# Two loads in flight instead of three at the start, and row sums kept in every second column

## The chip, the cores and the metric

One core of a Trainium2 chip runs the whole kernel. The metric is the device time of one execution in microseconds (us), as the median of several runs. The core's engines work side by side, each through its own list of instructions in order: PE (matrix products), DVE and POOL (vectors), ACT (functions and copies), and SP, which here only issues DMA transfers. They wait for each other through semaphores. TensorE and PE are the same engine.

## The reference: what is computed

Two attentions for each of 8 x 8 heads with 576 positions and 64 columns, one over means of four neighbours, one over a narrow band, and their sum goes into a feed-forward layer with `h * cos(h)`:

```python
q_d = q.reshape(B, H, Sd, 4, D).mean(axis=3)         # k_d, v_d alike; Sd = 144
out_up = np.repeat(sm_attn(q_d, k_d, v_d), 4, axis=2)
...
mask = np.abs(pos[:, None] - pos[None, :]) < 4
scores = np.where(mask, scale * q @ k.T, -1e9)
attn = np.exp(scores - max); attn = attn / (np.sum(attn, axis=-1, keepdims=True) + 1e-09)
x = (out_up + attn @ v) reshaped to [4608, 512]
...
h = x @ w_in                                          # w_in [512, 2048]
out = (h * np.cos(h)) @ w_out                         # w_out [2048, 512]
```

The weights arrive as float64 and everything else as float32.

## The kernel before, in words

**The feed-forward layer.** 4608 tokens stand in 12 tiles of 384 columns, the 2048 hidden columns in 16 chunks of 128. For a tile and a chunk, `gemm1` (L741) multiplies in 12 matmuls, each number being split in a high and a low part (h and l in the names), ACT and DVE form `h * cos(h)`, and `gemm2` (L777) adds the product with `w_out` to three PSUM banks in 9 matmuls. The first three tiles take turns, four chunks at a time, and the others come one by one with all 16 chunks.

**The weights.** Each chunk of `w_in` and of `w_out` is loaded by `w_load` (L410, 512 KB, names `wdi` and `wdo`). `w_split` (L420 to L432, then L399) makes float32 high and low parts out of the float64 bits on ACT, DVE and POOL, before gemm1 and gemm2 can read them (`wi`, `wo`).

**The attention.** It runs in 32 units, one for a batch and a pair of heads. A unit has five steps: `u_qk` loads q and k (L476, 292 KB each) and adds groups of four columns for the means (L490 on DVE, or L483 and L485 on POOL); `u_v` loads v twice (L497, 288 KB, names `vd`, and L498, 384 KB, names `vl`) and adds up the first one (L504, L505); `u_s` computes scores on PE (L539, L546, L555), subtracts maxima, applies the exponential and divides by row sums; `u_t` transposes (L634, L650); `u_pv` multiplies with v (L667, L679, L686), and L698, L713 and L399 write the result to the tiles x of the feed-forward layer. The units of the first two batches borrow buffers of weight chunks that come late, so in the rows their tiles carry names such as `wxi`, `wxo` and `xxl`.

**The row sums.** `su` is a tile of 16 columns, allocated in two copies. POOL sets it to 1 (L567). Twelve columns receive the sums of the local attention, four those of the other one (L610, or ACT's accumulator at L597). L612 adds a small number and scales, L614 takes the reciprocal, and L616 (or L622 on ACT) multiplies the rows by it.

**What sets the order.** A planner takes all operations with estimated durations, places them by due time and priority, and the instructions are emitted in that order; each engine follows its own list. Where PE would wait in the first 300 planned microseconds, it gets filling matmuls on an identity matrix (L916).

**The loads in flight.** All loads go out from SP's queue, in order. While the program is written, `dma` adds to each of the first `FIRST` = 40 loads a wait for the load `AHEAD` places before it, unless there is none yet. This dependency is added when the instruction is emitted, behind the planner's back: the planned order doesn't depend on it. SP takes its instructions in order, so a load that waits holds back every later one. The 40 loads are the q, k and v loads of the first two batches, the first four weight chunks in part, and one load of the third batch.

Of the kernel before, what the change touches and what calls it, by code (L numbers as in the profile page):

```python
# [24 lines left out]
P = 128  # L25
# [12 lines left out]
HD = SD // 2  # L38
# [3 lines left out]
NSEG = S // (4 * BQ)  # L42
# [7 lines left out]
ON_PE = ()  # L50
BOOST = {0: 100.0}
LAG = 2
AHEAD, FIRST = 3, 40
PI = math.pi


# [22 lines left out]
class Plan:  # L79
# [47 lines left out]
    def part(self, parent, off, n, make):  # L127

        b = self.buf(make)
        b.parent, b.prev = parent, []  # L130
        for lo, hi, p in parent.parts:
            if lo < off + n and off < hi:
                b.prev.append(p)
        parent.parts = [x for x in parent.parts if not (off <= x[0] and x[1] <= off + n)] + [(off, off + n, b)]
        return b
# [165 lines left out]
def attn_ffn_kernel(ctx: ExitStack, tc: tile.TileContext, qT, kT, vdn, vl, w_in, w_out, out):  # L301
    nc = tc.nc
    pe, act, dve, pool, sp = nc.tensor, nc.scalar, nc.vector, nc.gpsimd, nc.sync
# [6 lines left out]
    pl = Plan()  # L310

    def sb(tag, n, shape, dtype=F32, name=None, pool=None):
        t = pl.turn(tag, n)
        return pl.buf(lambda: (pool or ap).tile(shape, dtype, name=name or tag, tag=t, bufs=1), t)
# [195 lines left out]
    def u_s(b, pr):  # L510
# [49 lines left out]
            pl.op("PE", 1.55, lambda: (l_mm(), d_mm()), r=[q, k, qkd], pw=banks, w=loc + poo)  # L560


        mxl, su = sb("mxl", 2, [P, 2 * NSEG]), sb("su", 2, [P, 2 * NSEG + 4])
        sul = lambda: su.get()[:, :2 * NSEG]
        sud = lambda: su.get()[:HD, 2 * NSEG:].rearrange("p (a b) -> p a b", a=2)

        pl.op("POOL", 0.15, lambda: pool.memset(su.get(), 1.0), w=[su])  # L567
        for h in range(2):
            using(banks[h], pl.op("DVE", _dve(NSEG * BS), lambda h=h: dve.tensor_tensor(  # L569
                out=sml.get()[:, NSEG * h:NSEG * (h + 1)], in0=banks[h].get()[:, LQ:LQ + NSEG * BS].rearrange("p (s n) -> p s n", n=BS),  # L570
# [9 lines left out]
        for h in range(2):  # L580
            mx = pl.buf(None)
            using(banks[h], pl.op("DVE", _dve(2 * SD), lambda h=h: dve.tensor_reduce(
                out=mxd.get()[:, h], in_=dq(h), axis=AX.X, op=ALU.max, negate=early), r=[poo[h]], pw=[mxd], w=[mx]))
            if not early:
                using(banks[h], pl.op("DVE", _dve(2 * SD), lambda h=h: dve.tensor_tensor(
                    out=smd.get()[:, h], in0=dq(h), in1=mxd.get()[:, h].unsqueeze(2).broadcast_to([HD, 2, SD]), op=ALU.subtract),
# [21 lines left out]
        for sm, part, size in ((sml, sul, n), (smd, sud, m)):  # L608
            if not (early and sm is smd):
                pl.op("DVE", _dve(size), lambda sm=sm, part=part: dve.tensor_reduce(  # L610
                    out=part(), in_=sm.get(), axis=AX.X, op=ALU.add), r=[sm, su], pw=[su2])
        pl.op("DVE", 0.1, lambda: dve.tensor_scalar(out=su.get(), in0=su.get(), scalar1=1e-9, scalar2=2.0 * PI,  # L612
                                                    op0=ALU.add, op1=ALU.mult), r=[su2], w=[su])
        pl.op("DVE", 0.15, lambda: dve.reciprocal(su.get(), su.get()), w=[su])  # L614
        for sm, part, size, bc in ((sml, sul, n, bl), (smd, sud, m, bd)):
            f = lambda e, sm=sm, part=part, bc=bc: lambda: e.tensor_tensor(out=sm.get(), in0=sm.get(), in1=bc(part()), op=ALU.mult)  # L616
            alts = [("DVE", _dve(size), f(dve))]
# [193 lines left out]
    def unit(t, step, ahead, *a):  # L811
        for d, f in ((-ahead, u_qk), (0.01 - ahead, u_v), (0.0, u_s), (step, u_t), (2 * step, u_pv)):
            at(t + d, f, *a)

    for i in range(NPAIR):
        for t, f in ((-10.0 + 0.5 * i, u_qk), (-8.4 + 0.5 * i, u_v), (-7.5 + i, u_s), (-6.5 + i, u_t), (-5.5 + i, u_pv)):
            at(t, f, 0, i)
# [15 lines left out]
    for i in range(NPAIR):  # L833
        for t, f in ((-4.0 + 0.5 * i, u_qk), (-2.4 + 0.5 * i, u_v), (-0.9 + i, u_s), (-0.1 + i, u_t), (0.7 + i, u_pv)):
            at(t, f, 1, i)
# [124 lines left out]
```

## Time and profile before

| what | value |
|---|---|
| median of 3 timed runs | 1002.41 us (1001.95 to 1004.67) |
| the profiled execution, its own time | 1007.08 us |
| its span, first to last instruction | 1005.3 us |
| mean granted TensorE clock | 0.988 |
| PE busy | 985.1 us, 98% of the span |
| DVE / ACT / POOL busy | 67% / 61% / 22% |
| DMA moved | 80.70 MB |

The span is what lies between the first and the last instruction of the core; the execution's time has 1.8 us around it. Busy shares are means over stages that differ: in the first 107 us attention units, weight splitting and the first matmuls alternate on PE, later PE multiplies without a pause. In rows of instructions the first number is the start in microseconds from the beginning of the span, the second the duration of the row (of all its instructions together where it ends in x2 or more), then engine, line, operation, output <- inputs with shapes; square brackets hold the idle time of the engine before it and what ended it. Buffer numbers are left out of names.

### The profile page before, as it was taken

The numbers are of one execution on the slowest core, as the hardware profiler recorded it, in microseconds if no ns is written. First come the engines' busy times: TensorE is split into PE (matmuls) and PEld (weight loads), VectorE is DVE, ScalarE is ACT, GpSimd is POOL, SyncE is SP. The second block draws the span as 40 slices with busy tenths as digits, with TensorE's granted clock in tenths as the row PEclk, the third lists the DMA queues.
The fourth block names the chain that finished last, engine by engine and source line by source line (L and its number), as shares of the span: only waits on it lengthen the run. The fifth ranks groups of instructions, "written<-read, shape, count | busy, mean of one in ns | idle before, by whom it ended". The sixth has DMA issues, their size and how long they took to land.

```text
span 1005.3 us, 23882 instructions
## 1 busy us (share of the span) xinstructions
PE 985.1 (98%) x9932; PEld 850.3 (85%) x9932; DVE 678.2 (67%) x1362; ACT 610.2 (61%) x1174; POOL 223.8 (22%) x280
## 2 busy tenths in 40 slices
PE   8898999999998999999999999999999999999998
PEld 5556898899886888889888888888888888899997
DVE  7699999985686678464758957655657765433433
ACT  4357688876665656555547746654646665655554
POOL 6685334631242203000002211200001300000000
PEclk9699999999999999999999999999999999999999
DMA  7874733332453422210212412201112320100000
GB/s 230 250 249 159 255 119 62 72 59 45 75 131 105 84 66 70 66 33 28 82 48 71 127 49 58 82 26 36 64 52 73 116 60 4 37 1 1 32 1 32
DMA packets 41051, 80.70 MB, mean 80 GB/s; under 512 B 4976, under 2 KB 16240, under 8 KB 40944
## 3 DMA queue, kind: packets, MB, share of 16 engines
q1 hardware_dynamic: 37056, 72.11, 23.2%
q0 software_dynamic: 3888, 7.08, 5.0%
q8 instruction: 78, 1.28, 0.5%
q14 instruction: 29, 0.24, 0.1%
HBM read 57.93 MB, written 16.52 MB: 74 GB/s over the span
## 4 chain that ended last, share of the span: by engine, by line
PE 89%; DVE 5%; DMA 1%; issue 1%; ACT 1%; POOL 1%; SPq 0%; ACTq 0%; POOLq 0%; DVEq 0%
PE bank L777 38%; PE bank L741 38%; PE bank L539 2%; PE bank L916 2%; PE bank L686 2%; PE bank L555 2%; PE bank L667 2%; PE bank L650 1%; DMA q<-qT 1%; PE bank L679 1%; DVE su L610 1%; DVE xxh L421 0%; DVE tr L756 0%; PE bank L546 0%; DVE xxh L425 0%
## 5 line engine op out<-in xcount | busy, mean ns | idle before, releaser
L777 PE MATMUL bank<-wo,gh 128*128 128x512 f32 x1152 | 363.9, 397 | 0.0
L777 PEld LDWEIGHTS bank<-wo,gh 128*128 128x128 f32 x1152 | 210.2, 188 | 38.1 <-issue 3.2
L777 PE MATMUL bank<-wo,gl 128*128 128x512 f32 x576 | 227.7, 396 | 0.0
L752 ACT ACTIVATE tr<-bank,bmagic 128x384 f32<-128x384 f32 x192 | 110.9, 578 | 114.1 <-PE bank L741 109.2
L756 DVE SCALAR_TENSOR_TENSOR tr<-tr,bank 128x384 f32<-128x384 f32 x192 | 105.0, 547 | 108.1 <-ACT tr L751 107.4
L753 DVE SCALAR_TENSOR_TENSOR tr<-tr,bank 128x384 f32<-128x384 f32 x192 | 105.7, 551 | 82.8 <-ACT tr L752 81.8
L750 ACT ACTIVATE tr<-tr 128x384 f32<-128x384 f32 x192 | 100.6, 524 | 77.0 <-DVE tr L753 76.4
L758 ACT ACTIVATE gh<-tr 128x384 fp32r<-128x384 f32 x163 | 85.3, 523 | 91.9 <-DVE tr L756 90.1
L399 DVE TENSOR_TENSOR gl<-tr,gh 128x384 fp32r<-128x384 f32 x154 | 91.7, 596 | 63.5 <-ACT gh L758 59.8
L777 PEld LDWEIGHTS bank<-wo,gl 128*128 128x128 f32 x576 | 108.1, 188 | 23.5
L741 PE MATMUL bank<-x3h,wi 128*128 128x384 f32 x384 | 106.9, 338 | 1.6 <-DVE tr L756 1.0
L741 PE MATMUL bank<-x0h,wi 128*128 128x384 f32 x384 | 107.0, 339 | 0.0
L741 PE MATMUL bank<-x1h,wi 128*128 128x384 f32 x384 | 107.0, 339 | 0.0
L741 PE MATMUL bank<-x2h,wi 128*128 128x384 f32 x384 | 106.8, 339 | 0.0
L751 ACT ACTIVATE tr<-tr 128x384 f32<-128x384 f32 x192 | 100.9, 525 | 6.1
L399 POOL TENSOR_TENSOR gl<-tr,gh 128x384 fp32r<-128x384 f32 x38 | 43.3, 1139 | 268.2 <-DVE gh L759 174.7
L741 PEld LDWEIGHTS bank<-x3h,wi 128*128 128x128 f32 x384 | 70.2, 188 | 4.3 <-DVE tr L756 1.5
L741 PEld LDWEIGHTS bank<-x0h,wi 128*128 128x128 f32 x384 | 70.2, 188 | 2.4 <-DVE wxo L569 0.2
L741 PEld LDWEIGHTS bank<-x1h,wi 128*128 128x128 f32 x384 | 70.2, 188 | 2.4 <-issue 0.4
L741 PEld LDWEIGHTS bank<-x2h,wi 128*128 128x128 f32 x384 | 70.2, 188 | 2.2 <-DVE xxh L425 0.2
L741 PE MATMUL bank<-x3l,wi 128*128 128x384 f32 x192 | 64.6, 336 | 0.1
L741 PE MATMUL bank<-x0l,wi 128*128 128x384 f32 x192 | 64.5, 336 | 0.0
(199 smaller groups left out, 1457.2 us busy)
## 6 DMA issues: line engine op xcount, KB each, us to landing
vl<-vl SPq DMA_DIRECT2D x26, 384.0 KB
out<-ob SPq DMA_DIRECT2D x36, 256.0 KB
wdi<-w_in SPq DMA_DIRECT2D x16, 512.0 KB
wdo<-w_out SPq DMA_DIRECT2D x16, 512.0 KB
q<-qT SPq DMA_DIRECT2D x26, 292.0 KB
k<-kT SPq DMA_DIRECT2D x26, 292.0 KB
vd<-vdn SPq DMA_DIRECT2D x26, 288.0 KB
out<-ob POOLq DMA_DIRECT2D x27, 256.0 KB, 5.3
```

The lines of the kernel that those rows point to most:

```text
L399: f = lambda e: lambda: e.tensor_tensor(out=out(), in0=in0(), in1=in1(), op=ALU.subtract)
L539: pe.matmul(banks[h].get()[BS * g:BS * (g + 1), c:c + BS], q.get()[hs, o:o + BS], k.get()[hs, o:o + BS], start=True, stop=True)
L555: pe.matmul(banks[h].get()[:HD, i * SD:(i + 1) * SD], qkd.get()[hs, 0, i * HD:(i + 1) * HD], qkd.get()[hs, 1, :], start=True, stop=True)
L667: pe.matmul(banks[0].get()[64 * h:64 * h + 64, 2 * SD:3 * SD], vd.get()[:, kh, 64 * h:64 * h + 64], ptd.get()[:, h, kh, :], start=(kh == 0 ...
L741: pe.matmul(ph.get()[:, :m], w[:, i, kc, :], x[:, kc, :], start=(n == 0), stop=(n == 3 * KC - 1))
L750: act.activation(tr.get(), tr.get(), AF.Sin, scale=PI)
L751: return act.activation(tr.get(), tr.get(), AF.Square)
L752: pl.op("ACT", _act(m, True, 1), lambda: act.activation(tr.get(), h(), AF.Identity, bias=bmagic), r=[ph], w=[tr])
L753: pl.op("DVE", _dve(m), lambda: dve.scalar_tensor_tensor(out=tr.get(), in0=tr.get(), scalar=MAGIC, in1=h(), op0=ALU.subtract, op1=ALU.subt ...
L756: pl.op("DVE", _dve(m), lambda: dve.scalar_tensor_tensor(out=tr.get(), in0=tr.get(), scalar=0.5, in1=h(), op0=ALU.subtract, op1=ALU.mult), ...
L758: pl.op("ACT", _act(m, False), lambda: act.activation(gh.get(), tr.get(), AF.Copy), r=[tr], w=[gh], alts=[("DVE", _dve(m / 2), lambda: dve ...
L777: pe.matmul(o, (gh, gh, gl)[k].get()[:, sl], wo.get()[:, (0, 1, 0)[k]], start=(c == c0 and k == 0), stop=(c == c1 - 1 and k == 2))
```

## The change

It has two parts. `AHEAD` goes from 3 to 2: each of the first 40 loads waits for the second load before it. And `su` gets a third dimension of 2, so that the 16 sums stand in every second column of a tile of 32; all readers and writers of the sums use the view `every`, and only the memset of POOL writes the whole tile.

```diff
-AHEAD, FIRST = 3, 40
+AHEAD, FIRST = 2, 40
...
-        mxl, su = sb("mxl", 2, [P, 2 * NSEG]), sb("su", 2, [P, 2 * NSEG + 4])
-        sul = lambda: su.get()[:, :2 * NSEG]
-        sud = lambda: su.get()[:HD, 2 * NSEG:].rearrange("p (a b) -> p a b", a=2)
+        mxl, su = sb("mxl", 2, [P, 2 * NSEG]), sb("su", 2, [P, 2 * NSEG + 4, 2])
+        every = lambda: su.get()[:, :, 0]
+        sul = lambda: every()[:, :2 * NSEG]
+        sud = lambda: every()[:HD, 2 * NSEG:].rearrange("p (a b) -> p a b", a=2)
...
-        pl.op("DVE", 0.1, lambda: dve.tensor_scalar(out=su.get(), in0=su.get(), scalar1=1e-9, scalar2=2.0 * PI,
+        pl.op("DVE", 0.1, lambda: dve.tensor_scalar(out=every(), in0=every(), scalar1=1e-9, scalar2=2.0 * PI,
                                                     op0=ALU.add, op1=ALU.mult), r=[su2], w=[su])
-        pl.op("DVE", 0.15, lambda: dve.reciprocal(su.get(), su.get()), w=[su])
+        pl.op("DVE", 0.15, lambda: dve.reciprocal(every(), every()), w=[su])
```

The order of instructions is the same on every engine; the line numbers behind L563 are one higher after the change. What differs is what SP's loads wait for. The loads rotate over eight semaphores, DMAHW0 to DMAHW7, so the number tells which load is waited for. SP's list at its beginning (line, DMA, destination <- source, shape, and what it waits for), before:

```order
L476 DMA q<-qT 128x584
L476 DMA k<-kT 128x584
L476 DMA wxi_132<-qT 128x584
L476 DMA wxo_136<-kT 128x584 [waits DMAHW0_49]
L476 DMA wxo_203<-qT 128x584 [waits DMAHW1_49]
L476 DMA wxi_206<-kT 128x584 [waits DMAHW2_49]
```

and after the change:

```order
L476 DMA q<-qT 128x584
L476 DMA k<-kT 128x584
L476 DMA wxi_132<-qT 128x584 [waits DMAHW0_49]
L476 DMA wxo_136<-kT 128x584 [waits DMAHW1_49]
L476 DMA wxo_203<-qT 128x584 [waits DMAHW2_49]
L476 DMA wxi_206<-kT 128x584 [waits DMAHW3_49]
```

The third load used to go out at once and now waits for the first one (DMAHW0), and each later one waits for one load further on. The same list further down, where the loads of the second batch's v stand (`vd` and `vl` into borrowed tiles; the row with `wxi_312` and `-vdn` is load 32 when the first load is load 0), before:

```order
L410 DMA wdi_925<-w_in 128x4x256 [waits DMAHW1_49]
L410 DMA wdo_934<-w_out 128x1024 [waits DMAHW2_49]
L497 DMA vd_965<-vdn 72x1024 [waits DMAHW3_49,DVE_49,Pool_49]
L498 DMA vl<-vl 128x768 [waits DMAHW4_49,PE_49]
L497 DMA wxi_312<-vdn 72x1024 [waits DMAHW5_49,DVE_49,Pool_49]
```

and after the change:

```order
L410 DMA wdi_925<-w_in 128x4x256 [waits DMAHW2_49]
L410 DMA wdo_934<-w_out 128x1024 [waits DMAHW3_49]
L497 DMA vd_965<-vdn 72x1024 [waits DMAHW4_49,DVE_49,Pool_49]
L498 DMA vl<-vl 128x768 [waits DMAHW5_49,PE_49]
L497 DMA wxi_312<-vdn 72x1024 [waits DMAHW6_49,DVE_49,Pool_49]
```

Here too only the load that is waited for has moved on by one; the waits for DVE, POOL and PE, which free the buffers, are as before.

## The prediction

> **What bounds the kernel now.** First the page: its span, and the chain of work that ended last.
>
> ```profile
> span 1005.3 us, 23882 instructions
> ...
> PE 89%; DVE 5%; DMA 1%; issue 1%; ACT 1%; POOL 1%; SPq 0%; ACTq 0%; POOLq 0%; DVEq 0%
> ```
>
> PE is the chain. Next come the busy times by stretch: start and end, length, then busy time (and instructions) of PE, PE's weight loads, DVE, ACT and POOL, the granted clock, the share of time in which the DMA engines were busy, and GB/s.
>
> ```profile
> 0.75:57.11 56.36, 51.24 (x1058) 32.45 (x1058) 42.00 (x87) 23.08 (x78) 39.02 (x70) 0.82 0.83 243
> 95.00:105.00 10.00, 8.94 (x278) 5.59 (x279) 9.73 (x24) 6.39 (x15) 1.08 (x2) 1.00 0.94 334
> 45.00:50.00 5.00, 5.00 (x21) 2.11 (x18) 3.35 (x6) 1.97 (x5) 4.69 (x9) 0.50 0.82 221
> 107.20:1005.00 897.80, 889.70 (x7896) 787.56 (x7894) 587.17 (x1180) 553.03 (x1011) 153.05 (x173) 1.00 0.24 63
> ```
>
> From 107.2 us on, PE is busy for 889.70 of 897.80 us at full clock: matmul after matmul, in a fixed order. So the question is when PE reaches that stretch; a delay before it goes to the end whole, and nothing behind it can make it up. The 40 loads that the change touches are issued in the first 57 us. There the DMA engines are busy 0.83 of the time but move 243 GB/s, where the unlimited loads around 100 us move 334 GB/s. So the limit on loads in flight already holds the stream below what the engines can do.
>
> **What one load takes.** The rows below are issues on SP's queue (start, length). A load waits there for the third one before it, so an issue also tells when that one landed. Loads are counted from 0.
>
> ```profile
> 0.75 0.38 SPq L476 DMA_DIRECT2D q<-qT  x1
> ...
> 32.56 0.33 SPq L476 DMA_DIRECT2D xxl<-qT  x1
> ...
> 35.63 0.33 SPq L476 DMA_DIRECT2D wxi<-kT  x1
> ...
> 51.01 0.35 SPq L498 DMA_DIRECT2D wxi<-vl  x1
> ```
>
> ```profile
> 3.64 0.75 DVE L490 TENSOR_REDUCE qkd<-q 128x144 f32<-128x576 f32 x1 [2.76 <-DMA q<-qT]
> ```
>
> ```profile
> 78.92 0.32 SPq L497 DMA_DIRECT2D vd<-vdn  x1
> ...
> 82.40 1.32 POOL L504 TENSOR_TENSOR vd<-vd 72x512 f32<-72x512 f32 x1 [3.51 <-issue]
> ```
>
> Load 0 (292 KB) has gone out at 0.75 and DVE reads it at 3.64: 2.89 us. A 288 KB load that went out alone at 78.92 is used at 82.40: at most 3.48. With three in flight, load 35 goes out at 51.01, when load 32 has landed: 50.26 us for 35 loads, 1.436 each, so one load takes 3 x 1.436 = 4.31 us on average. Yet load 22, issued at 32.56, had landed when load 25 went out at 35.63: 3.07 us, with three in flight.
>
> **The change, part by part: loads.** No instruction is added or taken away, and the order on every engine stays. What changes is what a load waits for: the second load before it, not the third. Loads then run in two chains, the even and the odd ones, and each starts when its predecessor in the chain has landed. With T for the time of a load, even load 2n lands at 3.64 + nT. Three in flight need 4.31 / 3 = 1.44 us per load; two need T/2, and that is slower for every T over 2.87 us, so for every row above.
>
> T with two in flight isn't in the trace. It lies between 2.89, a load with little beside it, and 4.31, the average with two others beside it. I take 3.5: nearer to the lone loads, 2.89 to 3.48, because only one other load is left to share the engines with, and because the row of 3.07 shows that even three in flight need not cost more; above 3.48 because the chain also holds 512 KB loads.
>
> Early path. Load 12 is the first weight load, and ACT's queue holds it ahead of work for PE. ACT rows, then PE:
>
> ```profile
> 19.99 0.68 ACT L420 ACTIVATE xxh<-wdi 128x512 f32<-128x512 f32 x1 [0.18 <-DMA wdi<-w_in]
> 20.56 1.32 ACT L622 ACTIVATE wxi<-wxi,su 72x144 f32<-72x144 f32 x4
> ```
>
> ```profile
> 22.79 0.61 PE L650 MATMUL bank<-ident,wxi 72*72 72x72 f32 x4
> ```
>
> ACT waits for this load already now (0.18 us). Load 12 would land at 3.64 + 6 x 3.5 = 24.6, which is 4.6 late. Behind it in ACT's queue is L622, whose result PE transposes at L650; L622 ends at 21.88 and PE comes to it at 22.79, so 0.9 is absorbed: PE is 3.7 late, and everything on PE behind it.
>
> Later path. Load 32 is a `vd` load that POOL adds up at L504. POOL, then PE, then ACT:
>
> ```profile
> 52.08 1.38 POOL L504 TENSOR_TENSOR wxi<-wxi 72x512 f32<-72x512 f32 x1
> ...
> 60.72 0.27 POOL L567 MEMSET su<- 128x16 f32 x1 [0.54 <-DVE sml L616]
> ...
> 63.36 1.27 POOL L399 TENSOR_TENSOR wi<-xxh,wi 128x512 fp32r<-128x512 f32 x1 [0.16 <-ACT wi L431]
> ```
>
> ```profile
> 66.77 0.51 PE L741 MATMUL bank<-x0h,wi 128*128 128x384 f32 x2
> ```
>
> ```profile
> 68.73 0.57 ACT L752 ACTIVATE tr<-bank,bmagic 128x384 f32<-128x384 f32 x1
> 70.09 0.63 ACT L431 ACTIVATE wo<-xxh 128x512 fp32r<-128x512 f32 x1 [0.79 <-DVE xxh L427]
> ```
>
> POOL works without a pause from 52.08, and in its queue stands L399 at 63.36, the low half of the second weight chunk, which PE reads in the third matmul of gemm1 at 66.77. Load 32 lands at 51.0 now, 1.07 before use; at T = 3.5 it lands at 3.64 + 16 x 3.5 = 59.6 and POOL is 7.5 late. On the way 0.54 and 0.16 of POOL's waits are used up, then 66.77 - 64.63 = 2.14 in which the weight lay ready for PE, then 0.79 on ACT: 3.6 in all. What is left is 3.9. The two paths end in the same PE order, so the later one counts and they don't add: **+4**. Loads from 40 on go out without the limit, at up to the 334 GB/s of the row above, so I let them add nothing.
>
> **PE's clock.** PE will wait longer near 22 and near 67. Rows of the filling matmuls (L916):
>
> ```profile
> 12.06 2.33 PE L916 MATMUL bank<-ident_b 128*128 128x512 bf16 x10
> ...
> 46.21 5.17 PE L916 MATMUL bank<-ident_b 128*128 128x512 bf16 x14
> ```
>
> One takes 0.23 us at 12 us and 0.37 in the stretch that was granted 0.50. If the ten at 12 us ran at the other rate they would cost 1.4 more, and a second such group the same: from 0 to +2.8, less if a slow stretch turns fast instead. I take +1. The Trainium skill, "TensorE: Matmul & The Clock Gate", Part 1, says that an idle window of about 3.4 us halves the clock until one busy window has passed. The 0.50 above agrees with that; two such windows would add an estimated 3.4 us by the page, where I add 1.
>
> **The sums in every second column.** Rows of the tile view of `su` (count, shortest, median, longest in ns), and of a DVE instruction that reads every second column:
>
> ```profile
> L567 POOL MEMSET su<- x32: 106/112/431, 6.4 to 796.2; 128x16 f32 x32
> L612 DVE TENSOR_SCALAR su<-su x32: 156/164/1250, 16.4 to 849.9; 128x16 f32<-128x16 f32 x32
> L614 DVE RECIPROCAL su<-su x32: 203/248/254, 16.7 to 850.1; 128x16 f32<-128x16 f32 x32
> ```
>
> ```profile
> 40.70 0.68 DVE L425 SCALAR_TENSOR_TENSOR xxh<-wdo,xxh 128x512 int32<-128x512 int32 x1
> ```
>
> L425 takes 0.68 us for 512 columns, fixed part included: 1.3 ns a column, so 0.02 us for the 16 columns of L612 or L614 even if they took that on top. 64 such instructions make 1.3 us of DVE's time, 48 of them beside the stretch where PE doesn't wait; the 16 in the first 107 us make at most 0.3 us on a path. The memset writes 32 columns, not 16: at most double, 0.11 us, on POOL, which works 153 of the last 898 us. The readers of the sums (L616, L622) touch as many values as before. Bounds 0 and +0.4, by a cover that is PE itself; below nothing has no mechanism. I take 0.
>
> **Sum.** +4 for the loads, +1 for the clock, 0 for the sums: **+5**. The profiled execution took 1007.08 us, 1.8 more than its span, so it would take 1012. It is 4.7 over the median of the three timed runs, 1002.41; the change is the same for both, so the prediction is 1002.4 + 5 = **1007.4 us**.
>
> **Rivals.** *Two are enough.* If T is at most 3.1, load 32 lands by 53.2, which the 3.6 us absorb, and load 12 by 22.2, of whose 2.2 us PE sees 1.3. For it: 2.89 and 3.07. Against it: 3.48, and the weight loads. Time 1002.4 to 1003.7. The Trainium skill, "DMA: Bandwidth & Descriptors", section "Anatomy of one DMA — SWDGE (gpsimd) path", speaks for this case: about 2.0 us fixed plus bytes at 436 GB/s, given for another issue path than SP's. That is an estimated 2.69 us for 292 KB, by which load 32 would land at 46.7 and nothing would move. The measured 2.89 and 3.48 are 0.2 to 0.8 above it.
>
> *Each load keeps its time.* If T stays above 4.0, the cause of the 4.31 is not the third load but other traffic or the size. At 4.0 load 32 lands at 67.6, POOL is 15.5 late and 12 is left; at 4.31 it is 72.6 and 17. Time 1014 to 1019, with 1017 for the case. For it: the average itself. Against it: 3.07.
>
> *Faster.* PE stops for its own instructions where nothing in the profile holds it. Waits of PE in the first 100 us (total, times, longest):
>
> ```profile
> PE bank L679 <- issue: 1.8, 3, 1.0
> PE bank L546 <- issue: 1.6, 1, 1.6
> ```
>
> If these 3.4 us are instruction fetches that queue behind loads, fewer loads in flight shorten them; gone altogether, 1002.4 - 3.4 = 999.0. That decides only while no load is late, so for T up to about 3.0; against it, the fetch would have to be hindered by depth alone.
>
> **How the numbers follow.** Forecast (T from 3.1 to 4.0) 0.58, two are enough 0.22, each load keeps its time 0.15, faster 0.05. A measurement of this kernel tells about 0.3% from no change, 3.0 us. The loads pass +3 at T near 3.4, so I put 0.08 of the forecast's 0.58 within the bound. Slower 0.50 + 0.15 = 0.65, same 0.22 + 0.08 = 0.30, faster 0.05. The range takes in "two are enough" with the 0.5 us by which the lowest timed run lies under the median, so from 1001.8, and goes up to T = 4.0, +12, so to 1014.4. What it leaves out is the faster case and the upper part of the slowest one, some 0.15.
>
> **What would show it.** Load 12's ACT row (L420) starts near 24.6, the POOL row of load 32 near 59.6, load 39 goes out near 67 and not at 57, PE reaches its full stretch near 112, and that stretch is again about 898 us long. The DMA share in the first 57 us falls below 0.83 and GB/s below 243; if they hold, "two are enough" is right. The rows of L612 and L614 stay within 0.02 us. I am wrong if the long stretch itself changes, or if PE comes late where no load is.

## The result, and the profile after

| | kernel before | changed kernel |
|---|---|---|
| median of five runs each, same chip | 1002.41 us (1000.76 to 1005.43) | 1014.96 us (1014.33 to 1020.07) |
| ratio, 95% interval | | 1.0127 [1.0104, 1.0150] |
| the profiled execution, its own time | 1007.08 us | 1015.51 us |
| its span | 1005.3 us | 1013.7 us |
| mean granted TensorE clock | 0.988 | 0.981 |
| first matmul of the dense stretch | 107.18 us | 116.36 us |

The changed kernel is slower by 12.5 us; +5 was predicted, and the upper end of the range, 1014.4, is passed by 0.6. "Dense stretch" means here what begins with the 49th matmul of gemm1, from which on PE's waits that the profile lists make only some 4 us in all, in both kernels. Line numbers behind L563 are one higher in the changed kernel.

The page of the changed kernel, its span and its chain of work, then the busy times by stretch (columns as in the prediction: PE, PE's weight loads, DVE, ACT, POOL, granted clock, DMA share, GB/s):

```profile
span 1013.7 us, 23882 instructions
...
PE 85%; DVE 2%; DMA 1%; issue 1%; ACT 1%; POOL 1%; SPq 0%; ACTq 0%; DVEq 0%; POOLq 0%
```

```profile
0.75:57.11 56.36, 49.49 (x1044) 31.83 (x1045) 38.34 (x82) 20.88 (x69) 34.55 (x64) 0.79 0.67 193
75.00:80.00 5.00, 3.91 (x26) 3.47 (x30) 1.65 (x1) 0.98 (x2) 4.77 (x6) 0.50 0.97 310
116.30:1013.70 897.40, 890.14 (x7898) 789.09 (x7894) 588.95 (x1181) 553.18 (x1011) 152.38 (x173) 1.00 0.24 64
```

The dense stretch is as long as before, 897.40 against 897.80 us. Both of these executions have a window in it in which PE's granted clock was 0.50 (3.4 us from 316.5 before, 6.8 us from 312.2 after); in the traces of the twelve runs below it takes 893.4 to 894.7 us, whatever the loads do. In the first 57 us the DMA engines are busy 0.67 of the time (0.83 before) and move 193 GB/s (243). So the time was lost ahead of 116 us, in the stretch in which loads feed the attention. The two largest waits of PE there, and the largest one that ended with nothing that the profile shows ("issue"; total, times, longest in us):

```profile
PE bank L742 <- POOL wi L399: 5.3, 1, 5.3
PE bank L546 <- DMA k<-kT: 1.8, 1, 1.8
...
PE bank L668 <- issue: 0.8, 1, 0.8
```

The two rows "<- issue" that the prediction showed, at L679 and L546, are gone. Ahead of the dense stretch all waits of that kind make 1.0 us, against 4.3 in the kernel before.

The place of the early path, a row of ACT; then the later path: POOL from load 32 to the low half of the weight, PE's row behind it, and the issue of load 39 on SP's queue:

```profile
25.62 0.67 ACT L420 ACTIVATE xxh<-wdi 128x512 f32<-128x512 f32 x1 [3.16 <-DMA wdi<-w_in]
```

```profile
63.18 2.31 POOL L504 TENSOR_TENSOR wxi<-wxi 72x512 f32<-72x512 f32 x1 [7.18 <-DMA wxi<-vdn]
...
68.91 3.50 POOL L485 TENSOR_TENSOR wxi<-wxi,wxo 128x144 f32<-128x144 f32 x2
...
74.78 1.25 POOL L399 TENSOR_TENSOR wi<-xxh,wi 128x512 fp32r<-128x512 f32 x1
```

```profile
76.09 1.01 PE L742 MATMUL bank<-x0h,wi 128*128 128x384 f32 x2 [5.35 <-POOL wi L399]
...
79.59 0.62 PE L680 MATMUL bank<-sml,vl 32*64 32x24 f32 x16
```

```profile
72.49 0.33 SPq L476 DMA_DIRECT2D q<-qT  x1
```

POOL sits idle for 7.18 us until load 32 is there, starts 11.10 us later than before (63.18 against 52.08) and begins the weight's low half 11.42 later (74.78 against 63.36). PE stands still for 5.35 us before the third matmul of the second gemm1, which comes 9.32 later (76.09 against 66.77). Load 39 goes out 15.4 us later. The tile of the sums:

```profile
L568 POOL MEMSET su<- x32: 117/125/438, 6.4 to 803.9; 128x32 f32 x32
L613 DVE TENSOR_SCALAR su<-su x32: 154/165/1247, 19.6 to 858.3; 128x16 f32<-128x16 f32 x32
L615 DVE RECIPROCAL su<-su x32: 201/250/254, 19.9 to 858.5; 128x16 f32<-128x16 f32 x32
```

The medians have moved by 13 ns (memset), 1 ns and 2 ns.

### The profile page after: what moved, and what is told of

It is laid out like the page before. It is cut to its first block, busy times and chain, and to the rows that moved or that the text cites. A ratio compares the mean times of both kernels' runs of the same rounds, so it can differ in the third digit from the quotient of the medians.

```text
span 1013.7 us, 23882 instructions
## 1 busy us (share of the span) xinstructions
PE 989.0 (98%) x9932; PEld 854.4 (84%) x9932; DVE 676.2 (67%) x1362; ACT 610.3 (60%) x1174; POOL 224.6 (22%) x280
## 4 chain that ended last, share of the span: by engine, by line
PE 85%; DVE 2%; DMA 1%; issue 1%; ACT 1%; POOL 1%; SPq 0%; ACTq 0%; DVEq 0%; POOLq 0%
PE bank L778 39%; PE bank L742 38%; PE bank L539 2%; PE bank L687 2%; PE bank L555 1%; PE bank L668 1%; PE bank L651 1%; DMA ptb<-sml 1%; DMA q<-qT 1%; SPq L642 0%; DVE su L611 0%; DVE wo L399 0%; DVE tr L754 0%; POOL vd L504 0%; PE bank L917 0%
## 5 line engine op out<-in xcount | busy, mean ns | idle before, releaser
L754 DVE SCALAR_TENSOR_TENSOR tr<-tr,bank 128x384 f32<-128x384 f32 x192 | 105.7, 550 | 82.8 <-ACT tr L753 81.5
L399 DVE TENSOR_TENSOR gl<-tr,gh 128x384 fp32r<-128x384 f32 x154 | 93.0, 604 | 63.4 <-ACT gh L759 60.3
L399 POOL TENSOR_TENSOR gl<-tr,gh 128x384 fp32r<-128x384 f32 x38 | 44.9, 1182 | 271.6 <-DVE gh L760 185.3
L742 PE MATMUL bank<-x2l,wi 128*128 128x384 f32 x192 | 64.8, 338 | 0.0
```

The lines of the kernel that those rows point to most:

```text
L399: f = lambda e: lambda: e.tensor_tensor(out=out(), in0=in0(), in1=in1(), op=ALU.subtract)
L742: pe.matmul(ph.get()[:, :m], w[:, i, kc, :], x[:, kc, :], start=(n == 0), stop=(n == 3 * KC - 1))
L754: pl.op("DVE", _dve(m), lambda: dve.scalar_tensor_tensor(out=tr.get(), in0=tr.get(), scalar=MAGIC, in1=h(), op0=ALU.subtract, op1=ALU.subt ...
```

## The experiments

Each kernel is compared with runs of the kernel before on the same chip in the same session. Where a landing time of a load or the start of the dense stretch is given without a fence, it is read from that kernel's trace in the same way as above: the landing is the last increment of the load's semaphore, the start is that of the 49th matmul of gemm1.

### The two parts apart

`su_alone` is the changed kernel with three loads in flight:

```diff
-AHEAD, FIRST = 2, 40
+AHEAD, FIRST = 3, 40
```

> Three loads in flight, the sums in every second column. Theory A (the loads carry the whole change): within 3 us of the kernel before, 1002.4; L613 and L615 as long as L612 and L614 before, within 0.02 us. Rival B (the sums carry the part of 12.5 us that the two spans, 8.4 us apart, do not show): about 4 us slower, 1006.5.

Measured: 1004.82 us against 1003.28, ratio 1.0015 [0.9997, 1.0033]; load 32 lands at 49.51, the dense stretch starts at 107.23 (107.18 before). No effect shows. The rival's 4 us lie outside the interval, up to 0.33% does not.

`two_alone` is the kernel before with two loads in flight (and `two_again`, below, is the same kernel in another session):

```diff
-AHEAD, FIRST = 3, 40
+AHEAD, FIRST = 2, 40
```

> Two loads in flight, the sums as before. Theory A: the whole change, 1015.0, with load 32 landing near 63 us and PE waiting some 5 us for POOL's L399 near 71. Rival B: 1015.0 less the share of the sums, about 1011.

Measured: 1013.26 us, ratio 1.0098 [1.0072, 1.0124]; load 32 lands at 63.32, load 39 goes out at 72.23, the dense stretch starts at 115.33. The loads alone bring most of the loss, with the landings of the changed kernel. The wait of PE for L399, which the theory put at some 5 us, is 3.0 here; POOL's time behind load 32 differs between the two traces, as the table under "Which of the loads carry the delay" shows.

### How the time of one load depends on the number in flight

`one` and `four` set `AHEAD` to 1 and 4 in the kernel before.

> One load in flight for the first 40 loads, the sums as before. It measures the time of a lone load: theory A has 3.2 on average (2.9 to 3.5 seen for single loads), so load 32 lands near 3.6 + 32 x 3.2 = 106 and PE's dense start is some 50 us late, 1053. Rival F (the time of a load has nothing to do with the number in flight, 3.7 as with two): load 32 at 122, 66 us late, 1069.

> Four loads in flight, the sums as before. Theory A: T goes up by the same step as from two to three (3.7, 4.3, so 4.9), the stream gets 15% faster, load 32 lands near 45; but with three in flight the loads hold PE up nowhere in the chain, so the time stays within 3 us of 1003. Rival D (loads still hold PE up with three): 2 to 4 us faster. Rival E (the deeper queue hinders PE's instruction fetches): 2 us or more slower.

| in flight | mean time of a load, issue to landing, over the 40 | load 32 lands | dense stretch starts | ratio to before |
|---|---|---|---|---|
| 1 | 3.13 us | 103.97 | 164.76 | 1.0567 [1.0517, 1.0617] (two runs) |
| 2 (`two_alone`) | 3.70 | 63.32 | 115.33 | 1.0098 [1.0072, 1.0124] |
| 3 (before) | 4.34 | 50.95 | 107.18 | 1 |
| 4 | 4.93 | 45.76 | 111.46 | 1.0040 [1.0021, 1.0058] |

Each further load in flight adds some 0.6 us to the mean. With one, 33 loads in a row land at (103.97 - 0.75) / 33 = 3.13 us each, so the average load without any other limited load beside it already takes 3.13, not the 2.89 of load 0. The kind of load makes the difference: in `one` the q and k loads of 292 KB take 2.78 on average, v takes 3.36 (288 KB) and 3.10 (384 KB), and a weight load of 512 KB takes 3.75. The rival, in which the number in flight has no effect, had load 32 at 122. `one` took 1060.46 us: where the theory had 106 and 1053, load 32 landed at 103.97, and the time came out 7 us higher.

`four` is slower than three by 2.1 to 5.8 us, as rival E had it, although from load 3 to load 35 all its loads land earlier (those from 36 on land 2 to 4 us later). Waits of PE in its first 112 us; the prediction showed the same two rows with 1.8 and 1.6 us for the kernel before:

```profile
PE bank L679 <- issue: 3.4, 1, 3.4
PE bank L546 <- issue: 3.1, 1, 3.1
```

Here PE stops for nothing that the profile shows, for 6.5 us instead of 3.4. PE begins its first gemm1 at 56.41, against 52.64 before. POOL, whose load 32 landed at 45.76, comes to it only at 56.76:

```profile
47.10 1.00 POOL L399 TENSOR_TENSOR x0l<-wxo,x0h 128x384 fp32r<-128x384 f32 x1 [4.19 <-ACT x0h L713]
...
56.76 1.29 POOL L504 TENSOR_TENSOR wxi<-wxi 72x512 f32<-72x512 f32 x1
```

So what the rival "faster" supposed, that PE stops longer between its instructions when more loads are in flight, shows in the one trace with four. From three to two these stops shrink as well (4.3 us before, 1.0 in the changed kernel; 3.1 and 4.3 in the two traces with three all through, 1.0 to 3.4 in the six with two), which gives back less than the late loads cost. That the stops are fetches of instructions was not tested.

### Which of the loads carry the delay

`early2` limits the first 20 loads to two in flight and the rest to three, `late2` the other way round (the 2 and the 3 in the line of `ahead` change places), and `late33` lets only the loads from 33 on run with two (as `late2`, with 33 for 20). The edit of `early2`:

```diff
-                if len(begun) >= AHEAD:
-                    tc.add_manual_dep(ins.ins, begun[-AHEAD].name, mybir.DependencyInfo(
+                ahead = 2 if len(begun) < 20 else 3
+                if len(begun) >= ahead:
+                    tc.add_manual_dep(ins.ins, begun[-ahead].name, mybir.DependencyInfo(
```

> Only loads 0 to 19 wait for the second load before them, loads 20 to 39 for the third. Theory A (two paths end in PE's order, the later one counts, and each path has slack that is used up once): load 12 late by 5.6 us as in the changed kernel, the first gemm1 on PE some 3 us late, load 32 at about 37.5 + 13 x 1.44 = 56 to 57 us, so POOL's L504 4 to 5 us late, of which 3.6 are absorbed: +3 to +4, 1005.4 to 1006.4. Rival C (every load under the tighter limit costs its share, 12.5 / 38 = 0.33 us): 18 loads, +5.9, 1008.3.

> Loads 0 to 19 wait for the third load before them, loads 20 to 39 for the second. Theory A: the start up to 40 us is as before; load 32 lands at 30.6 + 7 x 3.72 = 56.6, 5.6 late, POOL's L504 4.6 late, 3.6 absorbed: +1, 1003.4; together with the other half far less than the whole 12.5. Rival C: 20 loads at 0.33, +6.6, 1009.

> Three in flight up to load 32, two only for loads 33 to 39. Theory (load 32, POOL's L504 behind it and the weight's low half in POOL's queue carry the delay): load 32 lands at 50 to 52 as before, load 39 goes out near 60 instead of 57, and the time is that of the kernel before within 1.5 us; dense stretch at 106.5 to 108. Rival (the loads of the last units count as well, since they too stand before POOL and DVE work): 2 to 4 us slower, dense stretch at 109 to 111.

Measured: `early2` 1007.96 us, ratio 1.0052 [1.0036, 1.0067]; `late2` 1006.65, ratio 1.0028 [1.0008, 1.0048]; `late33` 1003.91, ratio 1.0002 [0.9980, 1.0024]. In `late33` load 32 lands at 50.28 and load 39 goes out at 59.45, and no loss shows (more than 2.4 us is excluded), as the theory of load 32 had it. Against the kernel before in the same session, `early2` is 4.7 us slower, where the theory gave 3 to 4 and the rival 5.9; its interval, 3.6 to 6.7, holds both. `late2` is 3.4 us slower (0.8 to 4.8), where the theory gave 1 and the rival 6.6; this rules out the rival.

The three fit a slack that is used once: the halves move the dense stretch by 3.9 and 1.6 us, 5.5 together, where both at once move it by 8.1 in `two_alone`. (By the medians it is 4.7 + 3.4 against 10.0 us, which is not clear of the intervals.) The prediction's rule says: PE is late by what POOL's L504 is late, less 3.6 us. With 52.08 + 3.6 = 55.7 as the time up to which L504 costs nothing, and with the kernels of the next sections:

| kernel | POOL L504 of load 32 starts | rule: less 55.7 | POOL from L504 to the weight's low half | third matmul of the second gemm1 late by | dense stretch late by |
|---|---|---|---|---|---|
| before | 52.08 | 0 | 11.3 | 0 | 0 |
| `su_alone` | 50.39 | 0 | 11.2 | -1.5 | 0.0 |
| `late33` | 50.56 | 0 | 11.3 | -1.8 | -1.5 |
| `late2` | 56.11 | 0.4 | 9.7 | 0.4 | 1.6 |
| `early2` | 58.63 | 2.9 | 9.2 | 2.4 | 3.9 |
| `first30` | 59.82 | 4.1 | 12.7 | 7.1 | 7.9 |
| `pad2` | 61.16 | 5.5 | 11.6 | 7.3 | 8.2 |
| `two_again` | 61.85 | 6.2 | 9.4 | 5.8 | 9.2 |
| `after_again` | 62.28 | 6.6 | 11.6 | 8.4 | 10.5 |
| `view2` | 62.52 | 6.8 | 11.5 | 8.6 | 10.0 |
| changed kernel | 63.18 | 7.5 | 11.6 | 9.3 | 9.2 |
| `two_alone` | 63.39 | 7.7 | 9.5 | 7.5 | 8.1 |
| `one` | 104.03 | 48.3 | 10.1 | 48.7 | 57.6 |

Up to the third matmul the rule holds within 0.6 us where POOL takes 9.2 to 10.1 us from L504 to the weight's low half. In the five kernels in which POOL takes 11.5 us or more it is 1.7 to 3.0 us too low. So the landing of load 32 and the time that POOL then needs set PE together, and the rule left out that the second one varies. From the third matmul to the dense stretch the lateness changes by -0.1 to +2.1 us more, by 3.4 in `two_again`, where PE's clock was granted at 0.50 for the last 10 us ahead of it (105.7 to 115.9), and by 9 with one in flight. Each row is one execution (in `early2`, `late2` and `late33`, whose edit adds a line, L504 is L505).

### Load 32 brought forward, which did not help

`first30` has two in flight, but only for the first 30 loads; the others go out as soon as their buffers are free.

```diff
-AHEAD, FIRST = 3, 40
+AHEAD, FIRST = 2, 30
```

> Two loads in flight, but only for loads 0 to 29; from load 30 on no limit. Theory A (load 32, through POOL's queue, sets the delay): loads 30 to 32 go out together near 53 to 56, load 32 lands near 59 and not 63; POOL's L504 7 us late, 3.6 absorbed; dense start of PE 3 to 5 us late, 1007 to 1008. Rival C (a price for every limited load): 28 of 38 loads, about three quarters of the whole, 1010.5 to 1012.

Measured: 1014.30 us, ratio 1.0115 [1.0085, 1.0145]: as slow as `two_alone`. This expectation missed by 6 us or more. Load 32 did land earlier, at 59.76 instead of 63.32. POOL's rows, first of `first30`, then of `two_alone`:

```profile
59.82 3.65 POOL L504 TENSOR_TENSOR wxi<-wxi 72x512 f32<-72x512 f32 x1 [5.44 <-DMA wxi<-vdn]
...
66.92 3.06 POOL L485 TENSOR_TENSOR wxi<-wxi,wxo 128x144 f32<-128x144 f32 x2
...
72.53 1.26 POOL L399 TENSOR_TENSOR wi<-xxh,wi 128x512 fp32r<-128x512 f32 x1
```

```profile
63.39 2.16 POOL L504 TENSOR_TENSOR wxi<-wxi 72x512 f32<-72x512 f32 x1 [8.02 <-DMA wxi<-vdn]
...
68.98 1.40 POOL L485 TENSOR_TENSOR wxi<-wxi,wxo 128x144 f32<-128x144 f32 x2
...
72.93 1.25 POOL L399 TENSOR_TENSOR wi<-xxh,wi 128x512 fp32r<-128x512 f32 x1
```

POOL starts 3.57 us earlier and is done with the low half only 0.40 earlier. The same list of instructions, from L504 to the start of L399, takes 12.71 us instead of 9.54, almost all of it in L504 (+1.49) and the second pair of L485 (+1.66). DVE's rows at that time show where L504 was held, in `first30` and in `two_alone`:

```profile
61.93 0.42 DVE L423 TENSOR_SCALAR xxh<-xxh 128x512 int32<-128x512 int32 x1
62.26 0.57 DVE L634 STREAM_TRANSPOSE sml<-sml 128x384 f32<-128x384 f32 x1
62.76 1.27 DVE L427 SCALAR_TENSOR_TENSOR xxh<-wdi,xxh 128x512 int32<-128x512 int32 x1
```

```profile
64.00 0.42 DVE L423 TENSOR_SCALAR xxh<-xxh 128x512 int32<-128x512 int32 x1
64.34 0.57 DVE L634 STREAM_TRANSPOSE sml<-sml 128x384 f32<-128x384 f32 x1
64.83 1.27 DVE L427 SCALAR_TENSOR_TENSOR xxh<-wdi,xxh 128x512 int32<-128x512 int32 x1
```

L504 ends at 63.47 and 65.55, 1.21 us behind the start of DVE's transpose (62.26 and 64.34) in both, and alone it takes 1.26 (in `one`). So it seems not to have run until DVE came to L634. The same 1.21 us stand in the changed kernel, `after_again`, `pad2` and `view2`. Behind it DVE's L427 takes 1.27 us, where DVE's rows of the same operation and size take 0.62 to 0.68 in other places. The Trainium skill, "SBUF — State Buffer", section "SBUF: two separate sides", has a rule for this: DVE instructions with two inputs in SBUF, or in a mode that uses two ports, and POOL instructions that read SBUF hold one pair of ports for a whole instruction each, and the other one blocks. These rows agree with it, but for a RECIPROCAL of 0.24 us with one input that DVE ran at 60.76 in `first30`, without L504 getting in. It was read from traces, not tested with a kernel of its own. DVE's list is set by other things than load 32, so bringing that load forward moved POOL's wait to a place where DVE was in the way.

### Do the sums add anything when two are in flight?

The whole change had 12.5 us more than before, the loads alone 10.0 (9.8 by the ratio). `after_again` and `two_again` are these two kernels once more, in one session:

> The whole change once more, in the same session as the first part alone (two_again), to ask whether the sums in every second column add anything beside the loads. Theory (the loads are the whole effect): its median is within 3 us of two_again's, and the two intervals against the kernel before overlap. Rival (the sums cost as well, through DVE or POOL on the path): 2 to 4 us above two_again, as the single readings of 12.5 and 9.8 us would have it.

> Two loads in flight, sums as before: 1011 to 1015 us, ratio about 1.010 as the first time. Theory: equal to the whole change within the intervals. Rival: 2 to 4 us below it.

Measured: 1014.24 us, ratio 1.0105 [1.0073, 1.0137], and 1011.93 us, ratio 1.0089 [1.0056, 1.0122]. The intervals overlap, yet the whole change lies above the loads alone again, by 2.3 us. Two kernels split the second part, both with two in flight. `pad2` keeps the tile of 32 columns and the wide memset, with the sums side by side; `view2` keeps every second column, with a memset of these alone:

```diff
# pad2
-        every = lambda: su.get()[:, :, 0]
+        every = lambda: su.get().rearrange("p a b -> p (a b)")[:, :2 * NSEG + 4]
# view2
-        pl.op("POOL", 0.15, lambda: pool.memset(su.get(), 1.0), w=[su])
+        pl.op("POOL", 0.15, lambda: pool.memset(every(), 1.0), w=[su])
```

> Two loads in flight; the tile of the sums has 32 columns as in the whole change, which POOL's memset writes whole, but the 16 sums stand side by side in front. Two readings of the whole change lay 2.7 and 2.3 us above two readings of the loads alone. If the wider memset or the tile's place costs them: 1014 to 1015. If the access to every second column costs them, or nothing does: 1011 to 1013, as the loads alone.

> Two loads in flight; the sums stand in every second column as in the whole change, but POOL's memset writes only those 16 columns. If the strided access costs: 1014 to 1015. If the wider memset costs: 1011 to 1013. If the difference is a phase between POOL and DVE that any small shift turns over, pad2 and view2 fall on either value, and the POOL row L485 ahead of the weight's low half takes about 3.5 us for its two adds in a profile of a slow one and about 1.3 in a profile of a quick one.

Measured: 1012.35 us, ratio 1.0091 [1.0069, 1.0113], and 1013.43 us, ratio 1.0092 [1.0071, 1.0113]. Neither half stands out. The theory of a phase between POOL and DVE, with a slow pair of L485 in slow executions, did not hold: the pair took 3.13 us in the profile of `pad2`, whose execution was the quickest of its six (1010.49 us), and 1.20 in that of `two_again` (1012.14 us).

```profile
67.07 3.13 POOL L485 TENSOR_TENSOR wxi<-wxi,wxo 128x144 f32<-128x144 f32 x2
```

So the sums cost nothing that shows with three loads in flight, and beside two the medians leave 2.3 and 2.5 us, which the intervals do not separate from nothing. No row of theirs has a median longer by more than 13 ns. One difference goes with the wider tile: from L504 to the weight's low half POOL takes 11.5 to 11.6 us in the four kernels that have it and 9.4 to 9.5 in `two_alone` and `two_again`, through this pair of L485. Against it as the cause stand `first30` and `one`, whose tile has 16 columns and whose pair took 3.06 and 3.19, and `pad2`, whose median is no higher than those of the loads alone. It stays open.

## Why the prediction was wrong, point by point

**The bound.** Right: PE's dense stretch kept its length (897.40 against 897.80 us; within 1.4 us of each other in the twelve other traces) and carried the delay whole.

**Two chains.** Right: loads land in steps, and `one` to `four` show that the number in flight sets the landings.

**The time of a load.** This is the step that failed, in size. "I take 3.5", the prediction said, nearer to the lone loads of 2.89 to 3.48. Measured, load 32 landed at 63.12, which makes (63.12 - 3.64) / 16 = 3.72. The 0.22 us by which T was too low count 16 times, so load 32 came 3.5 us later than the 59.6 of the prediction; with the slack already used up, the term of +4 for the loads becomes +7.5 by the prediction's own rule. The lone loads were misleading: they are 292 KB and 288 KB, while the average with one in flight, `one`, is 3.13, and a second load adds 0.6. The row of 3.07 with three in flight, on which the choice of 3.5 leaned too, was a load of 292 KB as well. Even the rows of before would have given more: a straight line from 2.89 with one in flight to 4.31 with three gives 3.60 with two, and so 61.2 for load 32. The Trainium skill's figure, "DMA: Bandwidth & Descriptors", section "Anatomy of one DMA — SWDGE (gpsimd) path", by which the prediction estimated 2.69 us for 292 KB, lies 1.0 under the measured 3.72; it knows no other loads in flight. With one in flight, in `one`, loads of this size took 2.78.

**The early path.** Right in mechanism, and again 1.0 late: load 12's row on ACT stands at 25.62, not 24.6. PE begins the second gemm1 3.8 late (70.04 against 66.22), where 3.7 was predicted, and then stands still for POOL; so the early path does not add to the later one.

**The later path and its slack.** POOL was 11.10 late, where 7.5 was predicted. Of the 3.6 us of slack, POOL's own 0.70 was used up, but its adds took 1.02 us longer in all, by L504 and L485, for which the prediction had put nothing, so the weight came 11.42 late. PE's 2.14 were absorbed as predicted: 9.32 late at the third matmul. With the measured T the prediction's own rule gives 11.1 - 3.6 = 7.5 instead of 3.9.

**The clock.** Within its bounds where it was measured. From the third matmul of that gemm1 to L680 PE takes 79.59 - 76.09 = 3.50 us at a granted clock of 0.50. In the kernel before, the same stretch ended with this row, 1.82 after its beginning at 66.77:

```profile
68.59 1.11 PE L679 MATMUL bank<-sml,vl 32*64 32x24 f32 x62
```

That is +1.7 in one place; +1 was taken for the whole, from 0 to 2.8. Ahead of it PE is idle for 5.35 us, from 70.74 on, and the granted clock falls to 0.50 at 73.2. The rule of the Trainium skill, "TensorE: Matmul & The Clock Gate", Part 1, is that an idle window of about 3.4 us halves the clock. The trace agrees that idleness halves it, but the clock fell after 2.5 us; in the 3.4 us up to then (69.80 to 73.20) PE was busy for 0.94. PE is 11.0 late at L680, and 9.2 at the start of the dense stretch, so 1.8 is made up behind it.

**The sums.** The rows were right (within 2 ns on DVE, 13 ns on POOL), the price of 0 to 0.4 us is neither confirmed nor refuted, see above.

**The rivals.** "Two are enough" fell (T 3.72, not 3.1). "Each load keeps its time" gave 1014 to 1019 for T from 4.0, and the time came out there although T stayed under 4.0. "Faster" fell as a result, though the stops that it counted on did shrink, from 4.3 to 1.0 us; the late loads cost more.

**The sum.** With T = 3.72: 1002.4 + 7.5 + 1 = 1010.9, or +8.5. In the traces the dense stretch starts 9.2 late, 0.7 above this: POOL's adds (1.0) and the clock (0.7) came on top, and 1.8 was made up behind L680, in which the 0.79 of ACT may lie. The medians say more: +12.5 and +10.6 for the whole change, +10.0 and +8.3 for the loads alone. The sums may have a part in what is left, and the rest is not located. The two profiled executions differ by only 8.4 us, since that of before was itself 4.7 above its median; most of this lies in its dense stretch, 898 us where other kernels take 894. The second time of the changed kernel, 1014.24, lies just within the predicted range and the first just outside. That the loads took longer than the 3.5 us of the prediction holds in all six traces with two in flight: load 32 lands at 61.10 to 63.32, not at 59.6.

## What to carry to other kernels

A limit on loads in flight sets a chain, and its total is the time of one load times the number of links: an uncertainty of 0.2 us in one load is 3.5 us after 16 links, so take that time from the average over many loads and not from the quickest rows. Find the load whose reader has the least slack (here load 32, on POOL), use the slack once, because what it covers in one half of the chain is missing in the other, and don't take the reader's own time as fixed: POOL's differed by up to 3.5 us from kernel to kernel. The best depth has a loss on both sides: here two loads in flight were slower than three through late data, and four were slower too, with longer stops of PE for which the profile shows no cause.

## What the runs showed of the hardware that was not expected

The time of a load of some 350 KB on SP's queue grew almost evenly with the number in flight: 3.13, 3.70, 4.34 and 4.93 us for one to four. With more in flight PE waited longer for nothing that the profile shows: 3.4 us with three, 6.5 with four, in the same two lines (one trace each). A POOL instruction of 1.26 us took up to 3.65 us beside DVE, and ended 1.21 us after DVE came to a transpose, in six kernels alike. The granted clock of PE fell to 0.50 after 2.5 us without work.
